# Two heads' scores in turn, masks over 64 rows, and one scaling of all heads of a block

## The chip, the cores and the metric

The kernel runs on one core of one Trainium2 chip. The metric is device time in microseconds (us) of the whole program, the median of several runs. The core's engines are PE (TensorE: matmuls, with its weight loads shown as PEld), DVE (VectorE), ACT (ScalarE), POOL (GpSimd) and SP (SyncE, which issues the DMAs). They run side by side and wait for each other through semaphores; each takes its own instructions in a fixed order.

## The reference

```python
# attention with a memory: q, k, v are (8, 8, 576, 64)
scores = scale * np.matmul(q, k.transpose(0, 1, 3, 2))     # masked: keys after the query are left out
a = np.exp(scores - scores.max(-1, keepdims=True)); a /= a.sum(-1, keepdims=True) + 1e-09
local = np.matmul(a, v)
q_p = phi(q)                                               # x + 1 for x > 0, else exp(x)
mem_out = (q_p @ M_prev) / (q_p . z_prev + 1e-6)           # per head
attn = g * mem_out + (1 - g) * local                       # g = sigmoid(beta), per head
# FFN over all 4608 tokens, 512 -> 2048 -> 512
h = x @ w_in
out = (h * np.clip(h + 3.0, 0.0, 6.0) / 6.0) @ w_out
```

There are 8 sequences of 576 tokens and 8 heads of 64 columns; the FFN's weights come as float64.

## The kernel before

Attention is cut into units. A unit is one head and some 128-query blocks of one sequence: blocks 0 and 1 together, then 2, 3, and 4 (64 queries). A sequence has 32 units, in the order query blocks, pair of heads, head; there are 256. Keys lie on partitions, so a unit's scores fill one PSUM bank `sT`, of which three exist. A unit runs through these steps:

- `scores` (PE): L343 for sequence 0, whose q and k stay float32 with head 0 on partitions 0 to 63 and head 1 on 64 to 127, so that a product uses 64 rows of the array; L347 and L348 for the other sequences, in float16 parts over 128 rows. L350 adds the causal mask to the diagonal block, by a product of an identity with `negm` over 128 rows.
- `reduce`: the largest score per query, on DVE (L360; L358 on ACT for block 0) into `rm`, of which one exists, and then over the partitions on POOL (L362) into `mb`.
- `sub` (DVE, L368) into the tile `a`, of which two exist; `exp` (ACT, L377). From sequence 1 on, POOL makes the float16 upper part `ah` (L381) and DVE the lower `al` (L389, method `lo`).
- `pv` (PE): L407 and L408 for sequence 0, L413 to L417 otherwise. A group `o` in PSUM holds, for a block and both heads of a pair, the product with v, the one with the memory, and the two sums to divide by; two such banks exist.
- `combine`, after the second head of a pair: three small DVE operations make the factors `cf` (L430 to L432), four ACT operations scale the parts out of PSUM (L436, L437), a DVE addition (L438) puts 128 columns of `x` in place, and after the last pair `abs_sum` (L152) adds up magnitudes for the scaling of x.

The FFN works on 18 blocks of 256 tokens, each in 16 pieces: eight of the first product (L523 to L525, or L518 in float32 for block 0), followed by ACT and DVE operations (L531 to L534), and eight of the second (L546 to L548, or L544). Block 0's x is transposed on PE (L505), x of the others by DMA (L496). The weights are decoded from float64 on ACT and DVE (L622 to L626) during sequence 0 and split in float16 parts (L156, L157).

The pairs of the next sequence are prepared in ten steps each (load, magnitudes, scales, parts of k, q, phi(q) and v), whose temporaries come from the pools `hl` (three tiles) and `stg` (three).

The order in which each engine takes its instructions comes from a planner that lays out all instructions in a timeline of its own. An instruction's priority is the piece of the FFN at which it is wanted: `due(t)` for attention, 40 pieces ahead of the FFN (10 in the first 16 units), the piece's own number for the FFN, and fixed ones for the decoding of the weights. Loops only emit instructions; they don't set the order on an engine.

Of the kernel before, what the change touches and what calls it, by code (L numbers as in the profile page):

```python
# [67 lines left out]
def kernel(ctx, tc, qT, kT, v, mz, beta, w_in, w_out, out):  # L68
    nc = tc.nc
    PE, DVE, ACT, POOL, SP = nc.tensor, nc.vector, nc.scalar, nc.gpsimd, nc.sync  # L70
    B, NP, _, S = qT.shape          # 8, 4, 128, 576
    H = 2 * NP
    D = 64
    NT, DM = out.shape              # 4608, 512
    DFF = w_in.shape[1]             # 2048
    NB = 5                          # 128-token tiles per sequence (the last one has 64)
    TB = 256                        # tokens of an FFN block
# [13 lines left out]
    xpool = pool("xpool", XPB)  # L91
    ps_f = pool("ps_f", 2, space=PSUM)
# [11 lines left out]
    nat_eps = const.tile([P, 2], F32, name="nat_eps")  # L104
# [12 lines left out]
    for i in range(NSLOT):  # L117
# [9 lines left out]
        if i < NP:  # L127
            w32 = whole.bitcast(F32)
            nat.append(dict(q=w32[:, 0:S], k=w32[:, S:S + NB * P], qp=w32[:, S + NB * P:2 * S + NB * P],
                            v=w32[:, 2 * S + NB * P:2 * S + NB * P + NB * 130]  # L130
                            .rearrange("p (t h e) -> p t h e", t=NB, h=2)))
        else:
            raw.append(whole[:, 0:4096])

    def at(step):
# [18 lines left out]
    def split(hi, lo, src, s):  # L154
        """hi + lo = src * s, both float16."""
# [4 lines left out]
    slots = {}  # L160

    def prep_steps(b, p):
# [25 lines left out]
        def scale():  # L188
# [7 lines left out]
            DVE.memset(scal[:, 2:3], SA * 1e-9)  # L196
            DVE.tensor_scalar(scal[:, 3:4], s[:, 3:4], 1e-6, mem[b]["s"][:, 1:2], op0=ALU.mult, op1=ALU.mult)
            coef = mem[b]["coef"][:, 2 * p:2 * p + 2]
            DVE.tensor_scalar_mul(coef[:, :, 0], omg[:, 2 * p:2 * p + 2], i[:, 2:3])
            eps = scal[:, 2:4].unsqueeze(1).broadcast_to([P, 2, 2])  # L200
            esc, shift = scal[:, 0:1], scal[:, 1:2]
            slots[b, p] = dict(sl=sl, esc=esc, shift=shift, coef=coef, eps=eps)
# [23 lines left out]
        def do_phi():  # L226
            e = hl.tile([P, S], F32, name=f"e_{b}_{p}", tag="hl")
            q = st["q"][:, :S]
# [17 lines left out]
    def nat_load(p, part):  # L246
        """a pair of heads of sequence 0, for float32 products"""
# [12 lines left out]
    def nat_phi(p, part):  # L260
# [5 lines left out]
        coef = mem[0]["coef"][:, 2 * p:2 * p + 2]  # L266
        slots[0, p] = dict(esc=0.125, shift=8.0 * LN_SA, coef=coef,
                           eps=nat_eps.unsqueeze(1).broadcast_to([P, 2, 2]))

    def nat_mem():  # L270
# [8 lines left out]
        mem[0] = dict(t=m, coef=coef)  # L279
# [3 lines left out]
    def mem_steps(b):  # L283
# [16 lines left out]
        def conv():  # L300
# [7 lines left out]
            mem[b] = dict(t=t, s=s, coef=coef)  # L308
# [4 lines left out]
    # a unit: some 128-query blocks of one head, their scores in one PSUM bank, keys on partitions  # L313
    UNITS = [(0, 1), (2,), (3,), (4,)]
    xtiles = {}
    groups = {}

    class Unit:
# [10 lines left out]

        def scores(self):  # L330
            h = self.h
            if self.b == 0:
                t = nat[self.p]
            else:
                sl = slots[self.b, self.p]["sl"]
            sT = self.sT = ps_s.tile([P, 512], F32, name=f"sT_{self.id}", tag="sT")
            for i, nq, c0, _ in self.blocks:
                q0 = i * P
                for j in range(i + 1):
                    o = sT[:, c0 + j * nq:c0 + (j + 1) * nq]  # L340
                    if self.b == 0:
                        r = slice(D * h, D * h + D)
                        PE.matmul(o, t["k"][r, j * P:(j + 1) * P], t["q"][r, q0:q0 + nq],  # L343
                                  start=True, stop=j < i)
                    else:
# [463 lines left out]
```

## Time and profile before

| | |
|---|---|
| median of 3 runs | 1121.5 us (1119.45, 1121.5, 1121.78) |
| the profiled execution, first to last instruction | 1120.2 us |
| PE busy | 1083.2 us (97%) |
| DVE busy | 930.7 us (83%) |
| ACT busy | 791.1 us (71%) |
| POOL busy | 412.2 us (37%) |
| DMA | 101.39 MB, mean 91 GB/s |

The profiled execution's time is its span, 1120.2 us, which lies 1.3 us under the median and within the runs. Busy shares are unions of an engine's instructions. A matmul's record is longer than the time until the next one may start, so a busy PE says that it never stood idle for long, not that it works at its peak; the chain of waits, which gives to each instruction only the time until the next link, is the better measure of what one costs.

### The profile page before, as it was taken

Reading aid. Unit: us, or ns where it says so; the run is one execution under the profiler, and the core shown is the slowest. Engines: PE = TensorE matmul, PEld = TensorE weight load, DVE = VectorE, ACT = ScalarE, POOL = GpSimd, SP = SyncE. Lnnn points to the kernel's source line nnn. Section 1 sums busy time; section 2 is a strip of 40 time slices with the busy share of each in tenths; the row PEclk is TensorE's granted clock in tenths of the full one; section 3 lists DMA queues with packets and bytes.
Section 4 is the critical chain, followed back from the end, with each engine's and each line's share of the span. In section 5 each row is a group of like instructions: output and inputs, shape, how many; then the busy total and the mean of one; then the engine's idle time right before and its main releaser. Section 6 shows DMA issues by size and latency. Waiting matters only on the chain.

```text
span 1120.2 us, 28768 instructions
## 1 busy us (share of the span) xinstructions
PE 1083.2 (97%) x10736; PEld 797.4 (71%) x10736; DVE 930.7 (83%) x2436; ACT 791.1 (71%) x1880; POOL 412.2 (37%) x544
## 2 busy tenths in 40 slices
PE   8999999999999899999999999999999999999998
PEld 6888767586767667676768576867685868685664
DVE  5999889899899969998999988888799968893321
ACT  5787879677877778787877787668686857563321
POOL 3322223444444433554244533354344433341000
PEclk9999999999999999999999999999999999999999
DMA  8734452333424343315332434233404230101100
GB/s 263 291 100 160 119 135 70 94 91 87 116 84 106 70 118 89 97 45 138 97 76 71 101 96 102 76 92 97 116 22 107 77 69 14 36 5 36 27 13 19
DMA packets 101468, 101.39 MB, mean 91 GB/s; under 512 B 50256, under 2 KB 80976, under 8 KB 101328
## 3 DMA queue, kind: packets, MB, share of 16 engines
q1 hardware_dynamic: 101328, 99.56, 33.1%
q8 instruction: 84, 1.38, 0.5%
q14 instruction: 56, 0.46, 0.1%
HBM read 48.14 MB, written 9.44 MB: 51 GB/s over the span
## 4 chain that ended last, share of the span: by engine, by line
PE 42%; DVE 32%; ACT 8%; issue 8%; DMA 6%; POOL 2%; SPq 1%; DVEq 0%; ACTq 0%; POOLq 0%
DVE a L368 6%; PE po L546 5%; PE po L548 5%; PE po L547 5%; PE ph L523 5%; DVE rm L360 5%; PE ph L524 4%; PE ph L525 4%; DVE al L389 4%; DVE r L532 3%; PE ph L518 3%; DVE g L534 2%; PE sT L343 2%; DVE W L157 2%; POOL mb L362 2%
## 5 line engine op out<-in xcount | busy, mean ns | idle before, releaser
L362 POOL PARTITION_ALL_REDUCE mb<-rm x256 | 251.7, 983 | 336.7 <-DVE rm L360 237.4
L523 PE MATMUL ph<-x,W 128*128 128x256 f16 x1088 | 297.6, 274 | 12.7 <-DVE r L532 7.3
L525 PE MATMUL ph<-x,W 128*128 128x256 f16 x1088 | 297.5, 273 | 0.0
L524 PE MATMUL ph<-x,W 128*128 128x256 f16 x1088 | 297.4, 273 | 0.0
L381 POOL TENSOR_SCALAR_AFFINE_SELECT ah<-a 128x384 f16<-128x384 f32 (+2 forms) x224 | 145.4, 650 | 214.4 <-ACT a L377 105.4
L546 PE MATMUL po<-W,g 128*128 128x512 f16 x544 | 206.6, 380 | 1.9 <-ACT ot L554 1.6
L548 PE MATMUL po<-W,g 128*128 128x512 f16 x544 | 206.5, 380 | 0.8 <-DVE g L534 0.8
L547 PE MATMUL po<-W,g 128*128 128x512 f16 x544 | 206.7, 380 | 0.0
L377 ACT ACTIVATE a<-a,scal 128x384 f32<-128x384 f32 (+2 forms) x224 | 141.6, 633 | 57.0 <-DVE a L368 48.8
L368 DVE SCALAR_TENSOR_TENSOR a<-sT,scal,mb 128x128 f32<-128x128 f32 (+4 forms) x280 | 147.2, 541 | 13.3 <-POOL mb L362 12.4
L360 DVE TENSOR_REDUCE rm<-sT 128x128 f32<-128x256 f32 (+3 forms) x256 | 135.6, 530 | 11.5 <-PE sT L350 4.6
L389 DVE TENSOR_TENSOR al<-a,ah 128x384 f16<-128x384 f32 (+2 forms) x224 | 134.0, 598 | 9.2 <-POOL ah L381 8.0
L532 DVE SCALAR_TENSOR_TENSOR r<-r,ph 128x512 f32<-128x512 f32 x136 | 92.1, 677 | 53.2 <-ACT r L531 52.6
L436 ACT ACTIVATE x<-o,cf 128x64 f32<-128x64 f32 (+1 forms) x320 | 100.6, 314 | 44.2 <-DVE cf L432 39.5
L531 ACT ACTIVATE r<-ph,bias_g,gsc 128x512 f32<-128x512 f32 x136 | 106.5, 783 | 34.2 <-PE ph L525 29.1
L347 PE MATMUL sT<-slot 128*128 128x128 f16 (+1 forms) x840 | 123.7, 210 | 3.9 <-DVE a L368 2.1
L348 PE MATMUL sT<-slot 128*128 128x128 f16 (+1 forms) x840 | 124.3, 210 | 0.0
L523 PEld LDWEIGHTS <-W 128*128 128x128 f16 x1088 | 106.8, 98 | 23.1 <-issue 6.6
L413 PE MATMUL o<-slot,ah 128*128 128x65 f16 (+1 forms) x840 | 116.3, 195 | 6.9 <-ACT y L437 3.6
L533 ACT ACTIVATE g<-r 128x512 f16<-128x512 f32 x136 | 86.4, 636 | 51.2 <-DVE r L532 51.1
L524 PEld LDWEIGHTS <-W 128*128 128x128 f16 x1088 | 106.7, 98 | 19.5 <-issue 5.0
L414 PE MATMUL o<-slot,ah 128*128 128x64 f16 (+1 forms) x840 | 115.4, 195 | 0.0
(149 smaller groups left out, 2387.4 us busy)
## 6 DMA issues: line engine op xcount, KB each, us to landing
slot<-q SPq DMA_DIRECT2D x112, 144.0 KB, 2.5
out<-ot SPq DMA_DIRECT2D x36, 256.0 KB, 2.0
stv<-vn SPq DMA_DIRECT2D x28, 320.0 KB, 3.3
W<-w_in SPq DMA_DIRECT2D x8, 1024.0 KB, 9.5
slot<-w_out SPq DMA_DIRECT2D x8, 1024.0 KB, 4.9
stq<-qT SPq DMA_DIRECT2D x28, 288.0 KB, 3.1
stk<-kT SPq DMA_DIRECT2D x28, 288.0 KB, 3.3
slot<-k SPq DMA_DIRECT2D x112, 72.0 KB, 2.0
```

The lines of the kernel that those rows point to most:

```text
L360: DVE.tensor_reduce(rm[:, m0:m0 + nq], src.rearrange("p (t q) -> p q t", q=nq), axis=AX.X, op=ALU.max)
L362: POOL.partition_all_reduce(mb[:, 0:self.m], rm[:, 0:self.m], P, RMAX)
L368: DVE.scalar_tensor_tensor(a[:, c0:c0 + w].rearrange("p (t q) -> p t q", q=nq), self.sT[:, c0:c0 + w].rearrange("p (t q) -> p t q", q=nq), ...
L377: ACT.activation(a, a, AF.Exp, scale=slots[self.b, self.p]["esc"])
L381: POOL.affine_select(self.ah[:, 0:self.n], a, pattern=[[0, self.n]], compare_op=ALU.is_ge, fill=0.0, base=1, channel_multiplier=0)
L389: DVE.tensor_tensor(self.al[:, 0:n], self.a[:, 0:n], self.ah[:, 0:n], op=ALU.subtract)
L523: PE.matmul(ph[:, m], wh, f["xh"][:, c], start=c == 0, stop=False)
L524: PE.matmul(ph[:, m], wh, f["xl"][:, c], start=False, stop=False)
L525: PE.matmul(ph[:, m], wl, f["xh"][:, c], start=False, stop=c == 3)
L546: PE.matmul(po, gh[:, m, ts], W2[:, m, 0:512], start=m == 0, stop=False)
L547: PE.matmul(po, gh[:, m, ts], W2[:, m, 512:], start=False, stop=False)
L548: PE.matmul(po, gl[:, m, ts], W2[:, m, 0:512], start=False, stop=m == 15)
```

## The change

It has two parts. In sequence 0, the scores of the two heads of a pair are issued together: for each block and key tile a product of head 0 and one of head 1 in turn, into two `sT` banks. Their mask is added by products over 64 rows, two of 64 columns for a block of 128 queries, from the small tiles `selm` and `neg2`, which are built at the start in the free end of a slot. In the second part, `combine` no longer scales: one ACT copy per block and pair brings the whole group `o` into a tile `y` in SBUF, and after the last pair `normalise` makes the factors of all eight heads with three DVE operations and scales head by head, one ACT and one DVE operation each. The constants `eps` and `coef` stand per sequence for all heads, and two operations of a preparation move from DVE to ACT.

To make room, `rm` now stands in the first 256 columns of `a`, which is therefore taken at `reduce`; `hl` has two tiles and `x` three; phi's temporary is the staging tile of k; `y` has two tiles.

```diff
-HLB = 3
-XPB = 4
+HLB = 2
+XPB = 3
...
+        def scores_nat(self, other):
+            t = nat[self.p]
+            us = (self, other)
+            for u in us:
+                u.sT = ps_s.tile([P, 512], F32, name=f"sT_{u.id}", tag="sT")
+            for i, nq, c0, _ in self.blocks:
+                q0 = i * P
+                for j in range(i + 1):
+                    for u in us:
+                        r = slice(D * u.h, D * u.h + D)
+                        PE.matmul(u.sT[:, c0 + j * nq:c0 + (j + 1) * nq], t["k"][r, j * P:(j + 1) * P],
+                                  t["q"][r, q0:q0 + nq], start=True, stop=j < i)
+                for a in range(nq // D):
+                    for u in us:
+                        r = slice(D * u.h, D * u.h + D)
+                        c = c0 + i * nq + a * D
+                        PE.matmul(u.sT[:, c:c + D], selm[r, a, :], neg2[r, a, :],
+                                  start=False, stop=a == nq // D - 1)
...
         def reduce(self):
-            rm = p1.tile([P, 256], F32, name=f"rm_{self.id}", tag="rm")
+            a = self.a = p2.tile([P, 512], F32, name=f"a_{self.id}", tag="a")
+            rm = a[:, 0:256]
...
         def sub(self):
-            a = self.a = p2.tile([P, 512], F32, name=f"a_{self.id}", tag="a")
+            a = self.a
...
-                cf = small.tile([P, 2, 2], F32, name=f"cf_{self.id}_{i}", tag="cf")
-                DVE.tensor_tensor(cf[0:nq], g[0:nq, :, :, D], sd["eps"][0:nq], op=ALU.add)
-                DVE.reciprocal(cf[0:nq], cf[0:nq])
-                DVE.tensor_tensor(cf[0:nq], cf[0:nq], sd["coef"][0:nq], op=ALU.mult)
...
-                for h in range(2):
-                    ACT.activation(xs[:, h * D:(h + 1) * D], g[0:nq, h, 1, 0:D], AF.Copy, scale=cf[0:nq, h, 1:2])
-                    ACT.activation(y[:, h * D:(h + 1) * D], g[0:nq, h, 0, 0:D], AF.Copy, scale=cf[0:nq, h, 0:1])
-                DVE.tensor_tensor(xs, xs, y, op=ALU.add)
...
+                    ytiles[b, i] = ypool.tile([P, H, 2, D + 1], F32, name=f"y_{b}_{i}", tag="y")
+                y = ytiles[b, i]
+                ACT.activation(y[0:nq, 2 * p:2 * p + 2], groups[i][0:nq], AF.Copy)
+            if p == NP - 1:
+                for i, nq, _, _ in self.blocks:
+                    self.normalise(i, nq)
+
+        def normalise(self, i, nq):
+            b = self.b
+            y = ytiles[b, i][0:nq]
+            x = xtiles[b, i] = xpool.tile([P, DM], F32, name=f"x_{b}_{i}", tag="x")
+            cf = small.tile([P, H, 2], F32, name=f"cf_{b}_{i}", tag="cf")[0:nq]
+            DVE.tensor_tensor(cf, y[:, :, :, D], mem[b]["eps"][0:nq], op=ALU.add)
+            DVE.reciprocal(cf, cf)
+            DVE.tensor_tensor(cf, cf, mem[b]["coef"][0:nq], op=ALU.mult)
+            for h in range(H):
+                ACT.activation(y[:, h, 1, 0:D], y[:, h, 1, 0:D], AF.Copy, scale=cf[:, h, 1:2])
+                DVE.scalar_tensor_tensor(x[0:nq, h * D:(h + 1) * D], y[:, h, 0, 0:D], cf[:, h, 0:1],
+                                         y[:, h, 1, 0:D], op0=ALU.mult, op1=ALU.add)
+            abs_sum(amx[0:nq, b * NB + i:b * NB + i + 1], x[0:nq])
+            done_tiles.append((b, i))
...
+    DVE.memset(selm, 0.0)
+    for r in (slice(0, D), slice(D, P)):
+        DVE.tensor_copy(selm[r, 0, 0:D], ident[r, r])
+        DVE.tensor_copy(selm[r, 1, D:P], ident[r, r])
+        r0 = slice(r.start, r.start + 1)
+        DVE.memset(selm[r0, 0, 0:1], 0.0)
+        DVE.memset(selm[r0, 0, D:P], 1.0)
+        for a in range(2):
+            DVE.tensor_copy(neg2[r, a, :], negf[r, r])
+        DVE.memset(neg2[r0, 0, :], -3e38)
```

More of the change, by code (lines that the diff above doesn't have):

```diff
@@ L91 @@
     xpool = pool("xpool", XPB)
+    ypool = pool("ypool", 2)
     ps_f = pool("ps_f", 2, space=PSUM)
@@ L103 @@
     half = const.tile([P, 1], F32, name="half")
-    nat_eps = const.tile([P, 2], F32, name="nat_eps")
+    nat_eps = const.tile([P, H, 2], F32, name="nat_eps")
     W1 = const.tile([P, 17, 1024], F16, name="W1")
@@ L133 @@
             raw.append(whole[:, 0:4096])
+        if i == NP - 1:
+            free = whole.bitcast(BF16)[:, 2 * (2 * S + NB * P + NB * 130):]
+            selm = free[:, 0:2 * P].rearrange("p (a k) -> p a k", a=2)
+            neg2 = free[:, 2 * P:3 * P].rearrange("p (a q) -> p a q", a=2)
     def at(step):
@@ L195, in scale @@
             DVE.tensor_scalar(scal[:, 1:2], s[:, 0:1], s[:, 1:2], 8.0 * LN_SA, op0=ALU.mult, op1=ALU.mult)
-            DVE.memset(scal[:, 2:3], SA * 1e-9)
-            DVE.tensor_scalar(scal[:, 3:4], s[:, 3:4], 1e-6, mem[b]["s"][:, 1:2], op0=ALU.mult, op1=ALU.mult)
+            ACT.activation(mem[b]["eps"][:, 2 * p:2 * p + 2, 1], mem[b]["eps1"], AF.Copy, scale=s[:, 3:4])
             coef = mem[b]["coef"][:, 2 * p:2 * p + 2]
-            DVE.tensor_scalar_mul(coef[:, :, 0], omg[:, 2 * p:2 * p + 2], i[:, 2:3])
-            eps = scal[:, 2:4].unsqueeze(1).broadcast_to([P, 2, 2])
+            ACT.activation(coef[:, :, 0], omg[:, 2 * p:2 * p + 2], AF.Copy, scale=i[:, 2:3])
             esc, shift = scal[:, 0:1], scal[:, 1:2]
-            slots[b, p] = dict(sl=sl, esc=esc, shift=shift, coef=coef, eps=eps)
+            slots[b, p] = dict(sl=sl, esc=esc, shift=shift)
         def pair_tiles(nm):
@@ L226, in do_phi @@
         def do_phi():
-            e = hl.tile([P, S], F32, name=f"e_{b}_{p}", tag="hl")
-            q = st["q"][:, :S]
+            q, e = st["q"][:, :S], st["k"][:, :S]
             ACT.activation(e, q, AF.Relu, scale=-1.0)
@@ L265, in nat_phi @@
         DVE.scalar_tensor_tensor(e, q, 0.0, e, op0=ALU.max, op1=ALU.add)
-        coef = mem[0]["coef"][:, 2 * p:2 * p + 2]
-        slots[0, p] = dict(esc=0.125, shift=8.0 * LN_SA, coef=coef,
-                           eps=nat_eps.unsqueeze(1).broadcast_to([P, 2, 2]))
+        slots[0, p] = dict(esc=0.125, shift=8.0 * LN_SA)
     def nat_mem():
@@ L278, in nat_mem @@
         DVE.tensor_copy(coef[:, :, 1], gate)
-        mem[0] = dict(t=m, coef=coef)
+        mem[0] = dict(t=m, coef=coef, eps=nat_eps)
     mem = {}
@@ L307, in conv @@
             DVE.tensor_scalar(coef[:, :, 1], gate, s[:, 1:2], i[:, 0:1], op0=ALU.mult, op1=ALU.mult)
-            mem[b] = dict(t=t, s=s, coef=coef)
+            eps = small.tile([P, H, 2], F32, name=f"eps_{b}", tag="eps", bufs=2)
+            DVE.memset(eps[:, :, 0], SA * 1e-9)
+            eps1 = small.tile([P, 2], F32, name=f"eps1_{b}", tag="eps1", bufs=2)
+            DVE.tensor_scalar_mul(eps1, s[:, 1:2].broadcast_to([P, 2]), 1e-6)
+            mem[b] = dict(t=t, s=s, coef=coef, eps=eps, eps1=eps1)
         return [load, lambda: None, absmax, conv]
     UNITS = [(0, 1), (2,), (3,), (4,)]
-    xtiles = {}
+    xtiles, ytiles = {}, {}
     groups = {}
@@ L332, in scores @@
             if self.b == 0:
-                t = nat[self.p]
-            else:
-                sl = slots[self.b, self.p]["sl"]
+                if h == 0:
+                    self.scores_nat(self.pair)
+                return
+            sl = slots[self.b, self.p]["sl"]
             sT = self.sT = ps_s.tile([P, 512], F32, name=f"sT_{self.id}", tag="sT")
@@ L340, in scores @@
                     o = sT[:, c0 + j * nq:c0 + (j + 1) * nq]
[L341 to L345, printed above, removed]
-                        kk = kst[sl][:, h, j * P:(j + 1) * P]
-                        PE.matmul(o, kk, qhl[sl][:, 0, h, q0:q0 + nq], start=True, stop=False)
-                        PE.matmul(o, kk, qhl[sl][:, 1, h, q0:q0 + nq], start=False, stop=j < i)
+                    kk = kst[sl][:, h, j * P:(j + 1) * P]
+                    PE.matmul(o, kk, qhl[sl][:, 0, h, q0:q0 + nq], start=True, stop=False)
+                    PE.matmul(o, kk, qhl[sl][:, 1, h, q0:q0 + nq], start=False, stop=j < i)
                     if j == i:
@@ L666 @@
         nat_pads(p)
-    DVE.memset(nat_eps[:, 0:1], SA * 1e-9)
-    DVE.memset(nat_eps[:, 1:2], 1e-6)
+    DVE.memset(nat_eps[:, :, 0], SA * 1e-9)
+    DVE.memset(nat_eps[:, :, 1], 1e-6)
     ACT.activation(gate, beta_sb, AF.Exp, scale=-1.0)
@@ L699 @@
     NU = len(units)
+    for t in range(0, NU, 2):
+        units[t].pair = units[t + 1]
     upb = NU // B
```

9 lines of the change are left out of this document (removed).

## The prediction

> **What bounds the kernel now.** I read the page's busy shares first, then the windows by stage, then the chain of waits in the stage that the change touches most, then groups by form.
>
> ```profile
> span 1120.2 us, 28768 instructions
> PE 1083.2 (97%) x10736; PEld 797.4 (71%) x10736; DVE 930.7 (83%) x2436; ACT 791.1 (71%) x1880; POOL 412.2 (37%) x544
> 0.00:64.00 64.00, 58.34 (x237) 49.34 (x237) 49.82 (x132) 43.47 (x106) 21.57 (x25) 1.00 0.74 243
> 64.00:151.00 87.00, 86.87 (x500) 68.15 (x499) 78.77 (x192) 70.41 (x153) 22.81 (x24) 1.00 0.48 138
> 151.00:280.00 129.00, 120.34 (x1268) 86.54 (x1266) 119.09 (x311) 100.31 (x243) 54.28 (x70) 1.00 0.35 92
> 420.00:560.00 140.00, 136.73 (x1535) 102.54 (x1534) 132.16 (x365) 112.44 (x274) 60.09 (x80) 1.00 0.35 93
> 1000.00:1121.00 121.00, 114.44 (x865) 74.14 (x862) 37.97 (x83) 39.86 (x76) 6.07 (x11) 0.99 0.10 23
> ```
>
> The windows give length, then busy PE, PEld, DVE, ACT, POOL. From 64 us on PE is never idle for long: 86.87 of 87 us, later 93 to 98%. DVE is close behind (92% in 151 to 280, 94% in 420 to 560) until attention ends near 1000 us, and after that PE alone works. So PE work that disappears shortens the run, if DVE and the attention's buffers keep up; DVE work that disappears helps only through PE's waits.
>
> The chain from 64 to 151 us, sequence 0 beside FFN block 0, says the same:
>
> ```profile
> by line: PE ph L518 33.9%; PE sT L343 24.5%; PE o L407 16.4%; PE po L544 16.1%; PE o L408 3.6%; PE sT L350 2.8%; DVE a L368 1.1%; SPq L211 0.6%; SPq L210 0.6%; issue 0.3%; SPq L496 0.2%; DVE cf L432 0.1%; DVEq L368 0.0%
> 64.50 1.65 PE sT L343 x6
> 75.79 0.86 PE sT L343 x6
> 94.41 1.08 PE sT L343 x8
> 138.10 1.25 PE sT L343 x10
> 147.56 0.81 PE sT L343 x6
> 64.00:151.00 87.00, 23.64 (x150) 19.20 (x150) 1.00 0.48 138
> ```
>
> PE carries nearly all of it. L343, the scores of sequence 0, holds 24.5% of 87 us = 21.3 us, its mask (L350) 2.4 us. Columns are start, time on the chain, what; the last row is the window again, for L343 alone (its 150 matmuls and weight loads). Six instructions took 1.65 us at 64.5 but 0.86 at 75.8: in the first 70 us TensorE ran at half the speed, whatever the page's clock column (which says 1.00) shows.
>
> **Scores of sequence 0.** Read the cost of one from the chain: (1.08 - 0.86)/2 = 0.11 us per instruction, and 0.86 - 6 x 0.11 = 0.20 us to begin a piece. In the 64-column form of the last block (1.25 - 0.81)/4 is again 0.11, though the operand that streams is half as long. So what sets 0.11 there is not the streaming but, as far as the trace shows, the weight load that each instruction brings; and the 0.20 comes each time the array goes from 128-row work to these 64-row instructions.
>
> The change issues the two heads alternately, on partitions 0 to 63 and 64 to 127, into two PSUM banks, and keeps the mask at 64 rows too. Two terms:
> - 25 L343 pieces on the chain between 64 and 151 us (first 64.50, last 147.56, both above) become eight or nine pairs, some split. About 12 beginnings at 0.18 go: -2 us.
> - 150 instructions (the count in that window) at 0.11 = 16.5 us. If the two halves of the array work side by side this is 8.3 us less; if not, nothing. No row shows two halves at once. I take three quarters, -6, because of the 64-column form: an instruction whose streaming fills half its slot leaves the array waiting on its own half's weights.
>
> The Trainium skill, "TensorEngine Tiling (Array Packing)", Key Properties, says that tiles run weight loads and matmuls in parallel and that a change of tiling mode drains the engine; by it the second term is the full -8.3. The 0.20 us agrees with the drain; the parallel part no trace here shows. "TensorE: Matmul & The Clock Gate", Part 3, says that a weight load overlaps a running matmul only when the row group differs; 0.11 us for the 128-column form with one row group, loading and streaming in turn with no more than that between two starts, speaks against the word "only".
>
> The mask goes from one 128-column instruction per block and head to two of 64 columns. Before 17 of them took the 2.4 us, 0.14 each; after, an estimate of 0.1 per block in the same mode: -1 us; bounds -2 and +1. Scores together: -9 us, between -1 and -12. The scores before 64 us get cheaper too, but what PE waits for there is the x of FFN block 0 (last part); they count in the bounds of that step alone.
>
> The 15 small DVE instructions that build the masks come at the very start, where DVE is least busy (49.82 of 64 us in that window, most of it later). Nothing, or 1 us if the first mask waits.
>
> **Copies and scaling.**
>
> ```profile
> L437 ACT ACTIVATE y<-o,cf 128x64 f32<-128x64 f32 x256 | 82.6, 323 | 0.0
> L436 ACT ACTIVATE x<-o,cf 128x64 f32<-128x64 f32 x256 | 81.3, 317 | 35.6 <-DVE cf L432 30.8 <-DVE cf L431 2.0 <-PE sT L350 1.8
> L438 DVE TENSOR_TENSOR x<-x,y 128x128 f32<-128x128 f32 x128 | 39.6, 313 | 7.3 <-ACT y L437 7.0
> L432 DVE TENSOR_TENSOR cf<-cf,coef 128x4 f32<-128x4 f32 x128 | 27.4, 222 | 0.5
> L431 DVE RECIPROCAL cf<-cf 128x4 f32<-128x4 f32 x128 | 20.3, 167 | 0.4
> L430 DVE TENSOR_TENSOR cf<-o,scal 128x4 f32<-128x4 f32 x112 | 16.1, 151 | 6.6 <-PE o L417 6.4
> L199 DVE TENSOR_SCALAR coef<-omg,i 128x2 f32<-128x2 f32 x28 | 7.5, 268 | 0.0
> L197 DVE TENSOR_SCALAR scal<-s,s_m 128x1 f32<-128x1 f32 x28 | 5.6, 200 | 0.0
> L358 ACT ACTIVATE rm<-sT 128x128 f32<-128x128 f32 x64 | 17.8, 278 | 6.1 <-POOL mb L362 3.7 <-PE sT L350 2.2
> L377 ACT ACTIVATE a<-a,scal 128x320 f32<-128x320 f32 x56 | 31.3, 560 | 18.6 <-DVE a L368 14.5 <-POOL ah L381 2.5 <-DVE cf L432 1.1
> L377 ACT ACTIVATE a<-a,scal 128x512 f32<-128x512 f32 x56 | 40.5, 724 | 15.3 <-DVE a L368 12.4 <-DVE cf L432 1.9 <-DVE cf L431 0.7
> 41.94 0.20 ACT x L436
> PE o L413 <- ACT y L437: 3.6, 6, 1.3
> PE sT L347 <- DVE cf L430: 1.5, 1, 1.5
> PE ph L523 <- DVE r L532: 7.3, 7, 2.5
> ```
>
> DVE before: 151 + 167 + 222 + 313 = 853 ns for each of 160 pair-blocks, 136 us. After, for 40 blocks: three operations on 16 columns (0.55 us) and eight 64-column ones, for which there is no row; between 222 (L432) and 313 (L438, twice as long), nearer L438 as these have a pointer too: 290. 0.55 + 2.32 = 2.87 us, 115 us in all (93 to 122). With 28 x (200 + 268) = 13 us moved from the preparation to ACT, DVE loses about 34 us of 930.
>
> ACT before: four scalings, of which each holds the chain for 0.20 us (row at 41.94; they overlap), 0.8 x 160 = 128 us. After: one copy of 260 columns, 278 + 132 x (724 - 560)/192 = 391 ns, 63 us; eight scalings from SBUF per block, between 0.20 (that spacing) and 560 - 256 x 0.854 = 341 ns, say 0.25, 80 us; 56 small ones in the preparation, at that same 0.20, 11 us. ACT gains about 26 us and stays below 80%, so no cost by itself.
>
> What reaches PE: the waits for the output banks (3.6 us, L413 behind L437) and for cf (1.5) go, since a bank is free after one copy; what is late next is the 7.3 us in which PE waits for r, which DVE's relief trims a little and the new bursts (a block's eight pairs of operations in a row, two blocks at once for the first unit) lengthen. Net -5 + 3 = -2 us, between -8 and +8.
>
> **The shared tile a.** The maxima now stand in a, so a is taken at the reduction, not at the subtraction, and two exist.
>
> ```profile
> 91.16 1.11 PE L407 MATMUL o<-slot,a 128*128 128x65 f32 x8
> 86.69 0.67 DVE L360 TENSOR_REDUCE rm<-sT 128x128 f32<-128x512 f32 x1
> 93.36 0.67 DVE L368 SCALAR_TENSOR_TENSOR a<-sT,mb 128x512 f32<-128x512 f32 x1
> 100.59 1.11 PE L407 MATMUL o<-slot,a 128*128 128x65 f32 x8
> 447.44 0.55 DVE L360 TENSOR_REDUCE rm<-sT 128x128 f32<-128x384 f32 x1
> 447.91 0.55 DVE L389 TENSOR_TENSOR al<-a,ah 128x384 f16<-128x384 f32 x1
> 453.18 0.55 DVE L389 TENSOR_TENSOR al<-a,ah 128x384 f16<-128x384 f32 x1
> L362 POOL PARTITION_ALL_REDUCE mb<-rm x256 | 251.7, 983 | 336.7 <-DVE rm L360 237.4
> ```
>
> In sequence 0 the reduction at 86.69 ran 5.6 us before the product at 91.16 that frees its tile had ended (92.27); now it must follow, and with 0.67 + 0.98 + gaps its subtraction moves from 93.36 to about 94.3 to 94.9. The product it feeds started only at 100.59, PE having been given other work, so about 6 us cover this. Later the reduction at 447.44 starts 1.0 us before L389 two units earlier ends (448.46). It and its own L389 (end 453.73) lie 6.3 us apart: 3.15 us per unit with two tiles, against an average pace of about 1000/256 = 3.9 (attention fills the windows up to 1000 us, and L362 runs once per unit). That fits; behind a waiting reduction stand DVE's FFN operations, though. I take 0 as the cover exists; without it +1.5 us for each of ten rounds of sequence 0.
>
> **First x.** FFN block 0 waits for its x:
>
> ```profile
> 57.68 0.28 DVE L438 TENSOR_TENSOR x<-x,y 128x128 f32<-128x128 f32 x1
> 63.74 0.63 PE L505 MATMUL xp<-ident,x 128*128 128x128 f32 x2
> 66.16 2.45 PE L518 MATMUL ph<-x,W 128*128 128x256 f32 x5
> ```
>
> Of eight transposes only the last two (the row at 63.74) had to wait for the last pair; now all do (six more at about 0.2 us, 1.3 us), and for its scaling, whose 5.7 us replace 6.8 us spread earlier. +2 us (-3 to +5).
>
> The other edits: two hl tiles are enough since e moved to the staging tile, which is then kept two steps longer; one x tile less, but x is now taken only when finished. Cover: the steps of a preparation lie a unit, some 3.9 us, apart. SP's DMAs are the same in number; I count 0.
>
> **Sum.** 1120.2 - 9 - 2 + 0 + 2 = 1111.2 us of span; the median of the runs is 1.3 us above this span: 1112.5.
>
> **Rivals.**
> - Halves do not overlap: the second term is 0 and scores give -3; with -2 and +2 the run ends at 1118.5 or, with the bounds of the first x, 1116 to 1123. For it: 0.11 us looks set by weight loads, which have one queue. The same would be seen if the alternation only saved beginnings.
> - The tile a decides (slower). If the product is not 6 us but under 1.5 us behind the subtraction, each of ten rounds of sequence 0 costs 1.5 to 2 us, FFN block 0 runs out before x of block 1 is there, and in the sequences after it reductions stand 1 us late with DVE's queue behind them. 20 us of late attention less the 9 saved: 1121.5 + 11 = 1132. It decides once a unit's hold on a exceeds 2 x 3.9 us; 6.3 speaks against it, DVE at 94% for it.
> - DVE's relief counts fully: the 7.3 us of waits for r shrink too (-5 instead of -2), scores give -12, x is 3 us early: 1120.2 - 12 - 5 - 3 + 1.3 = 1101.5.
>
> **Chances.** Forecast 0.43 (own range 1106 to 1119), halves do not overlap 0.24, a decides 0.24, full relief 0.09. Repeats lie within 0.2% (1119.45 to 1121.78), which is what a measurement can tell from no change. Faster: 0.42 + 0.09 + a quarter of the second case = 0.56; same: half of the second and a little, 0.15; slower 0.29. Eight in ten: 1101 to 1132.
>
> **What would show it.** L343 pairs on the chain near 0.06 us per instruction: the overlap; 0.11: rival one. Subtractions of sequence 0 more than 1.5 us later after the product two units before, and a gap on PE between the last L544 and the first L523: rival two. ACT copies near 0.39 and 64-column DVE operations near 0.29 us check the copies. L518 starting in earnest after 70 us would break the first-x step; PE idle over 50 us between 151 and 840 would break the steady one.

## The result, and the profile after

The changed kernel takes 1131.24 us (median of 4 runs, 1129.75 to 1132.64), the kernel before 1120.47 us in the same comparison: ratio 1.0102, 95% interval 1.0082 to 1.0122. It is 1% slower; faster was forecast, 1112.5 us. The profiled execution has a span of 1128.0 us against 1120.2.

The page of the changed kernel (span, busy time by engine, the chain's shares by engine):

```profile
span 1128.0 us, 28530 instructions
PE 1078.5 (96%) x10768; PEld 795.4 (71%) x10768; DVE 925.4 (82%) x2181; ACT 797.4 (71%) x1776; POOL 400.1 (35%) x544
PE 44%; DVE 27%; ACT 10%; issue 8%; DMA 6%; POOL 3%; SPq 2%; DVEq 0%; ACTq 0%; POOLq 0%
PE po L575 5%; PE po L574 5%; PE po L573 5%; PE ph L550 5%; PE ph L551 5%; PE ph L552 5%; DVE a L382 4%; DVE a L390 4%; DVE al L411 4%; PE ph L545 3%; DVE r L559 2%; DVE x L465 2%; DVE g L561 2%; ACT y L464 2%; ACT a L399 2%
```

Busy totals hardly moved. The place of the loss is seen by stage. Windows of the kernel before and then of the changed one, cut at 228 and 242 us, where FFN block 2 begins (length, then busy PE, PEld, DVE, ACT, POOL, granted clock, DMA share, GB/s):

```profile
0.00:64.00 64.00, 58.34 (x237) 49.34 (x237) 49.82 (x132) 43.47 (x106) 21.57 (x25) 1.00 0.74 243
64.00:151.00 87.00, 86.87 (x500) 68.15 (x499) 78.77 (x192) 70.41 (x153) 22.81 (x24) 1.00 0.48 138
228.00:242.00 14.00, 14.00 (x184) 12.35 (x183) 14.00 (x29) 10.41 (x23) 6.59 (x8) 1.00 0.62 168
242.00:1000.00 758.00, 739.04 (x8327) 545.58 (x8325) 682.59 (x1817) 565.40 (x1378) 326.53 (x442) 1.00 0.32 81
```

```profile
0.00:64.00 64.00, 47.93 (x234) 44.14 (x234) 46.14 (x125) 40.64 (x92) 18.35 (x23) 1.00 0.73 243
64.00:151.00 87.00, 83.80 (x464) 65.96 (x465) 77.42 (x165) 70.10 (x145) 21.61 (x23) 1.00 0.44 133
228.00:242.00 14.00, 9.87 (x114) 7.83 (x113) 13.40 (x29) 9.52 (x19) 6.48 (x9) 0.76 0.54 139
242.00:1000.00 758.00, 739.64 (x8293) 544.58 (x8291) 674.56 (x1602) 569.42 (x1297) 316.99 (x438) 1.00 0.31 83
```

PE is busy 10.4 us less before 64 us, 3.1 less from there to 151, and another 4.1 less around 235 us, where the mean granted clock is 0.76. From 242 to 1000 us the two do alike. The start of FFN block 2 says it in one figure: its first product starts at 236.1 us against 227.8, 8.3 us later, and from there to the end both need 892 us (1128.0 - 236.1, 1120.2 - 227.8). Between these two executions the whole loss arises before block 2. PE's timeline of the kernel before and then of the changed one (in brackets the wait and what ended it):

```profile
227.81 0.27 PE L523 MATMUL ph<-x,W 128*128 128x256 f16 x1 [1.43 <-DMA x<-W]
```

```profile
236.05 0.37 PE L550 MATMUL ph<-x,W 128*128 128x256 f16 x1 [0.36 <-DMA x<-W]
```

Block 1's last product ends at 226.3 us before and at 228.3 now, so block 2 follows it after 1.5 us before and after 7.8 us now. In these 7.8 us PE does bits of attention until x of block 2 has come.

Two things are late there. First, attention of sequence 0. Windows again, for the products of its probabilities with v alone (PE, PEld; the trace has two instructions for each float32 product, 240 in all, and I count instructions here and below), of the kernel before (L407) and of the changed one (L429):

```profile
64.00:125.00 61.00, 12.08 (x88) 10.83 (x88) 1.00 0.43 138
```

```profile
64.00:125.00 61.00, 9.49 (x65) 8.76 (x65) 1.00 0.43 138
```

With those of the first 64 us (72 and 66), 160 have begun by 125 us before and 131 after. Unit 31 of sequence 0 ends at 178.2 us instead of 164.7. Second, x of FFN block 0. The waits of the changed kernel from 36 to 85 us (engine, line, releaser; us in total, times, longest) and PE's timeline there:

```profile
PE xp L532 <- DVE x L465: 3.7, 1, 3.7
DVE a L382 <- PE o L429: 2.4, 1, 2.4
```

```profile
62.17 0.63 PE L532 MATMUL xp<-ident,x 128*128 128x128 f32 x2
66.52 0.90 PE L532 MATMUL xp<-ident,x 128*128 128x128 f32 x3 [3.71 <-DVE x L465]
75.21 3.34 PE L545 MATMUL ph<-x,W 128*128 128x256 f32 x8
```

The transposes stand still for the scaling of all heads. Four instructions of block 0's products need only half of them; from the fifth on, all are needed. The fifth is my mark for the start of block 0: 75.2 us, against 66.2 before.

The parts of the change by themselves: the groups of the changed kernel (count, busy us, mean ns, idle before), and the chain of waits from 64 to 151 us.

```profile
L465 DVE SCALAR_TENSOR_TENSOR x<-y,cf 128x64 f32<-128x64 f32 (+1 forms) x320 | 75.8, 293 | 1.3 <-ACT y L464 1.2
L449 ACT ACTIVATE y<-o 128x260 f32<-128x260 f32 (+1 forms) x160 | 57.6, 376 | 37.4 <-PE o L439 32.2 <-PE o L430 3.8 <-DVE x L465 1.2
L346 PE MATMUL sT<-slot 64*128 64x128 f32 (+1 forms) x240 | 45.4, 352 | 14.9 <-DMA slot<-qT 4.4 <-issue 4.4 <-DVE a L390 3.4
```

```profile
82.69 0.03 PE sT L352
83.76 0.13 PE sT L352
84.84 0.06 PE sT L352 x2
93.32 1.09 PE sT L346 x8
97.53 0.86 PE sT L346 x6
105.50 0.64 PE sT L346 x4
```

Copy (376 ns) and scaling (293 ns) cost what was estimated. An instruction of the scores still takes (1.09 - 0.64)/4 = 0.11 us on the chain, as before: mostly, the two heads' products do not overlap. In the order that the planner gave to PE, one head's products mostly stand in a row and the other's follow later. A mask (L352) takes 0.03 us behind scores and 0.13 where it begins a piece.

### The profile page after: what moved, and what is told of

It reads as the page before. It is cut to its first block, busy times and chain, and to the rows that moved or that the text cites. A ratio compares the mean times of both kernels' runs of the same rounds, so it can differ in the third digit from the quotient of the medians.

```text
span 1128.0 us, 28530 instructions
## 1 busy us (share of the span) xinstructions
PE 1078.5 (96%) x10768; PEld 795.4 (71%) x10768; DVE 925.4 (82%) x2181; ACT 797.4 (71%) x1776; POOL 400.1 (35%) x544
## 4 chain that ended last, share of the span: by engine, by line
PE 44%; DVE 27%; ACT 10%; issue 8%; DMA 6%; POOL 3%; SPq 2%; DVEq 0%; ACTq 0%; POOLq 0%
PE po L575 5%; PE po L574 5%; PE po L573 5%; PE ph L550 5%; PE ph L551 5%; PE ph L552 5%; DVE a L382 4%; DVE a L390 4%; DVE al L411 4%; PE ph L545 3%; DVE r L559 2%; DVE x L465 2%; DVE g L561 2%; ACT y L464 2%; ACT a L399 2%
## 5 line engine op out<-in xcount | busy, mean ns | idle before, releaser
L384 POOL PARTITION_ALL_REDUCE mb<-a x256 | 239.2, 938 | 312.1 <-DVE a L382 247.6
L403 POOL TENSOR_SCALAR_AFFINE_SELECT ah<-a 128x384 f16<-128x384 f32 (+2 forms) x224 | 138.1, 617 | 247.6 <-ACT a L399 221.5
L399 ACT ACTIVATE a<-a,scal 128x384 f32<-128x384 f32 (+2 forms) x224 | 138.7, 622 | 61.5 <-DVE a L390 49.5
L411 DVE TENSOR_TENSOR al<-a,ah 128x384 f16<-128x384 f32 (+2 forms) x224 | 131.7, 589 | 27.8 <-POOL ah L403 26.8
L382 DVE TENSOR_REDUCE a<-sT 128x128 f32<-128x256 f32 (+3 forms) x256 | 135.9, 533 | 15.2 <-ACT a L380 6.6
L368 PE MATMUL sT<-slot 128*128 128x128 f16 (+1 forms) x840 | 120.4, 211 | 6.0 <-DVE a L390 5.1
L550 PEld LDWEIGHTS <-W 128*128 128x128 f16 x1088 | 106.6, 98 | 22.6 <-issue 4.4
L369 PE MATMUL sT<-slot 128*128 128x128 f16 (+1 forms) x840 | 121.6, 211 | 0.0
L551 PEld LDWEIGHTS <-W 128*128 128x128 f16 x1088 | 106.5, 98 | 16.0 <-issue 1.3
L552 PEld LDWEIGHTS <-W 128*128 128x128 f16 x1088 | 106.6, 98 | 11.8
```

Source lines behind the costliest of these rows:

```text
L382: DVE.tensor_reduce(rm[:, m0:m0 + nq], src.rearrange("p (t q) -> p q t", q=nq), axis=AX.X, op=ALU.max)
L384: POOL.partition_all_reduce(mb[:, 0:self.m], rm[:, 0:self.m], P, RMAX)
L399: ACT.activation(a, a, AF.Exp, scale=slots[self.b, self.p]["esc"])
L403: POOL.affine_select(self.ah[:, 0:self.n], a, pattern=[[0, self.n]], compare_op=ALU.is_ge, fill=0.0, base=1, channel_multiplier=0)
L411: DVE.tensor_tensor(self.al[:, 0:n], self.a[:, 0:n], self.ah[:, 0:n], op=ALU.subtract)
L550: PE.matmul(ph[:, m], wh, f["xh"][:, c], start=c == 0, stop=False)
```

## The experiments

Theory A: the scaling of all heads at once makes the first x of a sequence late (A2: of every sequence, not only the first). Theory B: tile `a`, taken at the reduction, slows attention. Rivals: the scores issued in pairs cost by themselves (C); the smaller pools cost (D); the order of issue costs, whatever the work (O). Each kernel's ratio is to the kernel before, with its 95% interval, from runs on the same chip.

**The parts alone.** e1_scores is the kernel before with the scores and masks of the change only.

> The first part of the change alone (scores of sequence 0 issued per pair of heads, masks over 64 rows), put into the kernel before; scaling, tiles and pools as before. Theory A (the loss is the late first x: scaling all heads at once holds up FFN block 0 by 9 us): nothing of that is in here, so 1118 to 1121 us, with the first long row of L518 at 64 to 67 us. Theory B (the tile a, taken at the reduction, slows the attention of sequence 0): the same, 1118 to 1121. Theory C (issuing the pair's scores together costs by itself, the second head waiting for a bank): 1125 or more, first FFN products later than 70 us.

1123.84 us, ratio 1.0029 (1.0013 to 1.0045), a time that none of the three had given. The part that was to bring 9 us costs 3. By 125 us 160 products have begun, like in the kernel before, so up to there attention runs neither slower nor faster. Block 2 starts at 226.8 us, 1.0 earlier than before: what this part costs lies after it.

e2_scaling is the rest of the change, with the scores of before.

> The second part alone: unscaled copies, scaling of all heads at once, with all that makes room for it (maxima in a, two hl tiles, three x tiles); scores and masks as in the kernel before. Theory A: all of the loss, 1129 to 1133 us, first dense FFN products at 73 to 77 us. Theory B: the same time. Theory C: 1119 to 1123 us.

1128.97 us, 1.0074 (1.0059 to 1.0089): most of the loss. e3_room takes only what made room: the maxima in `a`, two `hl` tiles, phi's temporary in the staging tile of k.

```diff
-            rm = p1.tile([P, 256], F32, ...)
+            a = self.a = p2.tile([P, 512], F32, ...)
+            rm = a[:, 0:256]
...
-HLB = 3
+HLB = 2
-            e = hl.tile([P, S], F32, ...)
+            q, e = st["q"][:, :S], st["k"][:, :S]
```

> Only what makes room: maxima in the first columns of a, hl with two tiles, phi's temporary in k's staging tile (x keeps four tiles, since it is taken at the first pair here); scaling per pair and scores as before. Theory A: no loss, 1119 to 1122 us, first FFN products at 64 to 68 us, though subtractions of sequence 0 come later. Theory B: 1127 to 1131 us, with the attention of sequence 0 some 10 us late at its end. Theory C: 1119 to 1122.

1129.66 us, 1.0081 (1.0066 to 1.0096). The room alone, without any of the new arithmetic, costs as much as e2.

e5_early is the changed kernel with blocks 0 and 1 of sequence 0 scaled pair by pair again.

```diff
+            if b == 0 and self.u == 0:      # four ACT scalings and a DVE addition per pair, from PSUM
+                ...
+                return
```

> The changed kernel with one exception: blocks 0 and 1 of sequence 0 are scaled pair by pair out of PSUM as in the kernel before, all other blocks at once. Theory A: FFN block 0 gets its x early again, dense products from 65 to 68 us, and the time falls by 7 to 10 us to 1120 to 1124. Theory B: the attention stays late, 1128 to 1132. Theory C: 1128 to 1132.

1134.10 us, 1.012 (1.0105 to 1.0135), and block 0's products still start at 74.0 us. Late scaling of the first x is not what holds the changed kernel, as long as everything else stays; theory A by itself falls. The time is 2 us above what theory B gave.

**Tile a.** e7_max_in_a has only the first part of e3's edit, e8_hl only the others.

> One edit to the kernel before: the maxima stand in the first columns of a, which is thereby taken at the reduction. Theory B (tile a): nearly all that the room cost, 1126 to 1131 us, block 0 of the FFN ending at 150 to 155 us while the product of unit 23 ends at 140 us or later (125.0 before), and PE without FFN work in between. Theory D (the loss of the room came from the two hl tiles or from phi's temporary): 1119 to 1122 us.

> The rest of the room alone: two hl tiles and phi's temporary in k's staging tile; the maxima in their own tile as before. Theory B: 1119 to 1122 us. Theory D: 1126 to 1131 us.

e7: 1135.94 us, 1.0136 (1.0104 to 1.0168). e8: 1121.43 us, 1.0000 (0.9985 to 1.0015). So the pools by themselves are free, and what the room costs comes with tile `a`. The parts don't add up, though: e7 is one of e3's edits and costs more than e3 (1.0081), and more than the whole change. Then e14_a3 gives e7 a third tile `a`.

```diff
-            a = self.a = p2.tile([P, 512], F32, name=f"a_{self.id}", tag="a")
+            a = self.a = p2.tile([P, 512], F32, name=f"a_{self.id}", tag="a", bufs=3)
```

> Kernel before with the maxima reduced into tile a (as in e7_max_in_a, which was 1.36% slower) but with three tiles a instead of two. Theory B (the ring of two tiles a is what the early taking costs): the third buffer gives the two rounds of cover back, so within 0.3% of before (1117 to 1124 us), and attention of sequence 0 as before (unit 23 ended near 121 to 129 us against 142.8 in e7). Rival (e7 was slow for the order of issue that the planner made of it, not for the ring): still 1130 to 1138 us.

1121.91 us, 0.9995 (0.9977 to 1.0013): the cost is gone. The windows of the products with v, as above, of e7 and then of e14:

```profile
0.00:64.00 64.00, 17.85 (x66) 16.28 (x66) 1.00 0.74 243
64.00:125.00 61.00, 7.47 (x54) 6.80 (x54) 1.00 0.43 138
```

```profile
0.00:64.00 64.00, 18.02 (x72) 16.52 (x72) 1.00 0.74 243
64.00:125.00 61.00, 11.22 (x80) 10.33 (x80) 0.92 0.37 124
```

120 products by 125 us against 152. The ring of two tiles, held from the reduction on, is a cause, and it is shown on the unchanged arithmetic. The start of block 2 does not show it: 237.0 us in e7, 237.2 in e14. But in e7 it is 9.5 us after block 1's end, in e14 0.8 us, and in e14 attention is further on by then (48 instructions of line L416, the lower parts' products with v, against 36), so that less is left to do: 882.4 us from there to the end against 897.3. The start of block 2 is a good mark of lateness only beside these two.

**Does the array overlap two heads?** e6_forced_scores is e1 with the alternation fixed on PE.

```diff
+            def mm(*args, **kw):            # each product of the two heads is issued after the one before
+                with tc.issue_after(last[0].ins):
+                    last[0] = PE.matmul(*args, **kw)
```

> The kernel with the scores' part alone, with each score product of a pair and each mask product bound to follow the one before it in the order of issue, head 1 first, so that the two halves of the array really alternate on PE (in the changed kernel's own order the heads mostly come one after the other). If the halves work side by side: near 0.06 us per L343-type instruction (0.55 us for a pair's first 8), and 1112 to 1119 us. If weight loads keep them in turn: 0.11 us each as before, and 1119 to 1126 us, PE waiting where a second bank comes late.

1131.27 us, 1.0093 (1.0059 to 1.0127). PE's timeline of the changed kernel (one head) and then of e6 (two heads in turn), eight instructions of 128 columns each:

```profile
81.54 1.16 PE L346 MATMUL sT<-slot 64*128 64x128 f32 x8
```

```profile
100.25 0.72 PE L348 MATMUL sT<-slot 64*128 64x128 f32 x8
```

Eight take 0.72 us instead of 1.16. In e6's trace they start two by two, 7 ns apart, one for each half of the array, and 0.11 us lie between two such pairs. So the halves work side by side, PE does the scores nearly twice as fast, and the kernel is still 0.9% slower, slower than either expectation: unit 23 ends at 149.5 us, against 125.0 before. A likely reason, which I did not test, is that a pair now starts only when two `sT` banks are free at once. PE's time was not what attention lacked.

**The cure of B in the changed kernel.** e9_after_mb reduces the maxima in place in `mb` and takes `a` at the subtraction again.

```diff
-            a = self.a = p2.tile([P, 512], F32, ...)
-            rm = a[:, 0:256]
             mb = self.mb = p2.tile([P, 256], F32, ...)
+            rm = mb
```

> The changed kernel with the maxima written into mb and reduced there in place, so that a is taken at the subtraction again; all else as changed. Theory B: most of the loss goes, 1119 to 1125 us, unit 23's product ends before 132 us (141.1 in the changed kernel). If the scaling at once or the pair of scores were the cost instead: 1128 to 1133 us.

1134.63 us, 1.0137 (1.009 to 1.0183). Attention of sequence 0 is fast again (180 products by 125 us, the fifth instruction of block 0 at 61.3 us), and nothing is gained: the waits have moved. Here theory B alone falls too. e13_mb does this edit on the kernel before, e10_scaling_mb on e2.

> Kernel before with the maxima reduced into tile mb and the all-reduce done in place, so that the single tile rm no longer makes a reduction wait for the all-reduce before it; tile a as before. If e9_after_mb was slow for this way of holding the maxima: 1126 to 1136 us here too. If it was slow for the scaling of all heads at once: here 1115 to 1122 us, same as before or up to 0.4% faster, with unit 31 of sequence 0 ended near 155 us as in e9 (154.1; before 164.7).

> Copies and scaling of all heads at once alone (e2_scaling) with the maxima in mb instead of a; scores as before. Theory B alone (tile a was all that e2 lost): 1117 to 1123 us. Theory A2 (scaling all heads at once makes the x of the first tiles of every sequence late, so that FFN block 2 starts near 237 us instead of 228, and similar gaps follow at later sequences): 1127 to 1134 us, as e9.

e13: 1129.21 us, 1.0061 (1.0038 to 1.0083), so holding the maxima in `mb` costs the kernel before 0.6%, which I had not expected. e10: 1134.70 us, 1.0135 (1.0096 to 1.0175), 0.7% beyond e13. Scaling at once costs something where `a` does not hold attention back. e12_pairs_mb tests that: e9, but blocks 0 and 1 of every sequence scaled pair by pair out of PSUM (four tiles `x`, one `y`).

```diff
+            if self.u == 0:
+                ...
+                    ACT.activation(xs_h, g[0:nq, h, 1, 0:D], AF.Copy, scale=cf[0:nq, h, 1:2])
+                    DVE.scalar_tensor_tensor(xs_h, g[0:nq, h, 0, 0:D], cf[0:nq, h, 0:1], xs_h, ...)
+                return
```

> e9_after_mb with blocks 0 and 1 of every sequence scaled pair by pair straight from PSUM, as the kernel before does, and the other blocks all heads at once (four tiles x, one tile y). Theory A2: the first x of a sequence comes early again, FFN block 2 starts before 230 us, and the time is 1118 to 1126 us. Rival (many small waits of another order of issue, none of them the first x): 1130 to 1136 us as e9, whatever block 2 does.

1115.96 us, 0.9943 (0.9921 to 0.9965): 18.7 us less than e9, faster than the kernel before, and 2 us below what theory A2 gave. The window at block 2 of e9 and then of e12:

```profile
228.00:242.00 14.00, 9.97 (x82) 6.83 (x81) 13.12 (x26) 7.93 (x19) 7.59 (x7) 0.76 0.67 160
```

```profile
228.00:242.00 14.00, 12.67 (x164) 10.46 (x162) 13.54 (x23) 9.94 (x17) 8.40 (x9) 1.00 0.59 148
```

Block 2 holds the last 64 tokens of sequence 0 and the first 192 of sequence 1, so it needs x of that sequence's first two query blocks. It starts at 236.8 us in e9 and 231.8 in e12, 6.3 and 1.1 us after the end of block 1. In the 16 us up to block 4 and up to block 13, in each of which the first query block of another sequence is wanted, PE waits for 3.5 and 3.6 us in e9, for 0.4 and 0.2 in e12. So scaling at once does delay blocks, where attention isn't late already. That is theory A2, with two reserves: the tiles `x` and `y` changed in number along with it, and these delays are the smaller part of the gain. The expected mark, block 2 before 230 us, was missed, and from block 2 to the end e12 needs 879.8 us against 897.6 in e9 and 892.4 in the kernel before. Why the rest is so much shorter is open; 11 us of it are less idle time of PE (11.8 us after the start of block 2 against 22.8).

**Both undone, and each put back.** e16_pairs_rm is e12 with `rm` as a tile of its own again; e18_pairs_a has the maxima in `a`; e19_pairs_noscores is e16 with the scores of before.

> e12_pairs_mb with the maxima in a tile rm of their own again, as in the kernel before; so the changed kernel with both suspected costs undone: tile a is taken at the subtraction, and blocks 0 and 1 of every sequence are scaled pair by pair from PSUM (one tile y, four tiles x). Theory (A2 and B are what the change lost, and mb in place cost 0.6% in e13): 1105 to 1114 us, 0.6 to 1.4% faster than before. Rival (e12 gained by a lucky order of issue): 1116 to 1125 us.

> e16 with the maxima in tile a (two of them) as in the changed kernel. Theory B: some 1.0 to 1.4% slower than e16, 1118 to 1130 us, attention of sequence 0 late (unit 23 ended after 138 us). Rival (with the rest cured, PE has cover enough): within 0.4% of e16.

> e16 with the scores and masks of sequence 0 as in the kernel before. If the scores part gains nothing or loses its 0.3% (e1_scores): 0 to 0.4% faster than e16. If the cheaper masks gain here what they could not in e1: 0.2 to 0.5% slower than e16.

e16: 1124.69 us, 1.0028 (1.0012 to 1.0044). e18: 1131.01 us, 1.0083 (1.0063 to 1.0103). e19: 1141.13 us, 1.0171 (1.0136 to 1.0207). B holds again: 6.3 us between e16 and e18, 160 products by 125 us against 121. e18 is no faster than the changed kernel (1131.24), so with `a` as it is the early scaling is worth nothing, as in e5. (Of e19's runs, 1134 to 1147 us, the profiled one is the shortest.) All three expectations failed in part. e16 does not beat the kernel before, and e12's way of holding the maxima, which cost e13 0.6%, is worth 8.7 us here. The difference of e18 to e16 is 0.6%, where 1.0 to 1.4 was expected. And the scores part, which costs 0.3% alone, gains 1.4% in e16 over e19. In e19 block 2 starts at 241.3 us (231.0 in e16), with PE and its clock down:

```profile
228.00:242.00 14.00, 6.68 (x82) 4.96 (x82) 13.69 (x31) 10.21 (x22) 7.97 (x9) 0.71 0.40 92
```

```profile
228.00:242.00 14.00, 12.70 (x153) 10.69 (x151) 14.00 (x26) 10.14 (x17) 8.76 (x11) 0.80 0.57 140
```

**Is it the order of issue?** Three kernels with the same work and another order: the kernel before with 41 pieces of lead (e21_order_lead) or the preparation two pieces later (e22_order_po), and the changed one with 41 (e23_after_order).

```diff
-LEAD = 40
+LEAD = 41
```

> Kernel before with one figure of the order of emission altered: attention runs 41 pieces of the FFN ahead instead of 40. The same instructions and tiles; about half of the streams of all engines stand in another order. If the planner's order alone scatters the time of this kernel by some 0.5% (theory O): anywhere from 1115 to 1132 us, more than 0.2% from before. If order alone is worth little: 1118 to 1123 us.

> Kernel before with the preparation of the next pairs two pieces later (10 instead of 8), everything else equal. Theory O: 1115 to 1132 us, more than 0.2% from before, in either direction. If order alone is worth little: 1118 to 1124 us.

> The changed kernel with 41 pieces of lead instead of 40. If its loss is a matter of the order that the planner came to: between 1118 and 1138 us, off from 1131.2 by more than 3 us. If the loss is in the tiles (theory B and the late x): 1129 to 1133 us, whatever the order, and unit 23 of sequence 0 still ends after 138 us, block 2 of the FFN after 234 us.

Ratios 0.9988 (0.9968 to 1.0008), 1.0002 (0.9985 to 1.0019) and 1.0115 (1.0082 to 1.0149). Although about half of PE's instructions stand elsewhere in the first two, neither differs from the kernel before, and e23 keeps the loss with its marks: 132 products by 125 us, block 2 at 237.3 us. (Its time, 1134.25 us, is 1 us above the range given for a loss in the tiles, but the ratio agrees with the changed kernel's 1.0102.) These small shifts of order are worth 0.2% at most on the kernel before. The loss goes with the tiles.

| kernel | ratio | products with v by 125 us | block 1 ends, us | block 2 starts, us | from there to the end, us |
|---|---|---|---|---|---|
| before | 1 | 160 | 226.3 | 227.8 | 892.4 |
| changed | 1.0102 | 131 | 228.3 | 236.1 | 891.9 |
| e1, scores alone | 1.0029 | 160 | 225.1 | 226.8 | 896.3 |
| e7, maxima in a | 1.0136 | 120 | 227.5 | 237.0 | 897.3 |
| e14, three tiles a | 0.9995 | 152 | 236.4 | 237.2 | 882.4 |
| e9, cure of B | 1.0137 | 180 | 230.5 | 236.8 | 897.6 |
| e12, e9 scaled early | 0.9943 | 170 | 230.7 | 231.8 | 879.8 |
| e16, both cures | 1.0028 | 160 | 219.9 | 231.0 | 889.2 |
| e18, a put back | 1.0083 | 121 | 226.7 | 236.0 | 893.4 |

## Why the prediction was wrong, step by step

- **What bounds the kernel.** "PE work that disappears shortens the run, if DVE and the attention's buffers keep up" failed before 228 us, by its condition. PE is nearly always busy there, but FFN block 0 and attention share it, and block 2 cannot start before x of sequence 1, whose way leads through DVE, ACT, POOL and DMAs. In e16 block 0's last second product ends at 158.7 us, 11 us earlier than the 169.7 of before, yet block 1 starts only at 165.4 and block 2 at 231.0: what PE gained it waited out.
- **Scores, -9 us.** The step that failed is "the change issues the two heads alternately". The loops emit them so; the planner mostly did not keep it. So 0.11 us stayed, the sign of the first rival, though not for its reason: the disputed overlap itself is real (0.72 us for eight in e6). Instead of -9 us the part alone measured +3 (e1), and where the overlap was forced, +11 (e6). The Trainium skill, "TensorEngine Tiling (Array Packing)", Key Properties, lets tiles load and multiply in parallel: e6 agrees, at (0.72 - 0.27)/7 = 0.064 us between starts, where 0.27 us is one record of the kind in e6; two of them, on different halves, start 7 ns apart. The Trainium skill, "TensorE: Matmul & The Clock Gate", Part 3, lets a weight load overlap a running matmul only in another row group, and e6 beside the 0.11 us of one row group fits that too. No row shows how long a load or a stream takes by itself, so the 0.11 us, which the prediction held against the word "only", is no evidence against it. The mask term was right: 0.03 us in most places and 0.13 at the start of a piece, against 0.14 before.
- **Copies and scaling, -2 us.** The prices held: 376 ns for the copy (391 forecast), 293 for DVE's 64 columns (290), some 0.25 us between ACT's scalings. DVE's relief did not: 34 us forecast, 930.7 - 925.4 = 5.3 us measured. I had added mean durations, but short records overlap their neighbours, as DVE's timeline of the kernel before shows (start, length, count):

```profile
301.58 0.22 DVE L430 TENSOR_TENSOR cf<-o,scal 128x4 f32<-128x4 f32 x2
301.77 0.25 DVE L431 RECIPROCAL cf<-cf 128x4 f32<-128x4 f32 x2
301.98 0.24 DVE L432 TENSOR_TENSOR cf<-cf,coef 128x4 f32<-128x4 f32 x2
302.14 0.35 DVE L368 SCALAR_TENSOR_TENSOR a<-sT,scal,mb 128x128 f32<-128x128 f32 x1
```

  Six operations fill 302.14 - 301.58 = 0.56 us, 0.09 each, where the groups' means (151, 167 and 222 ns) gave 1.08. ACT rose by 6.3 us (26 forecast), in the main for the same reason: of the 57.6 us of the new copies, other records of ACT cover 18.
- **Tile a, 0 us.** This is the step that turned the sign. Alone it measured +15.5 us (e7), and 6.3 us between e16 and e18. Rival two had the mechanism. That its 1132 us is the time measured is luck: it is a sum of 20 us of late attention, where 13.5 were measured at unit 31, less 9 us saved by the scores, which never came. "About 6 us cover this" took one wait for slack. In sequence 0 the rows that I quoted give a hold from the subtraction at 93.36 to the end of the product at 100.59 + 1.11 = 101.70, 8.3 us, already beyond the 2 x 3.9 us at which I had said that it decides; the 6.3 us that "speaks against it" came from the float16 units at 447 us. (By the pace of sequence 0 itself, 5.0 us per unit over its last eight, two tiles allow 10.0 us; with reduction and all-reduce the hold is 8.3 + 0.67 + 0.98 = 9.95 us, at the limit without any gap.) With reduction and all-reduce in the hold the ring sets the pace. The traces show it unit by unit: from the third unit of sequence 0 on, the kernel before starts 23 of 30 reductions before the product two units earlier has ended; the changed kernel, e7 and e18 start none of the 30 before it, and e14, with three tiles, 22. For unit 15 of the changed kernel:

```profile
82.65 0.88 PE L429 MATMUL o<-slot,a 128*128 128x65 f32 x6
85.87 0.55 DVE L382 TENSOR_REDUCE a<-sT 128x128 f32<-128x384 f32 x1
```

  Unit 13's product ends at 82.65 + 0.88 = 83.53 us, and the reduction that takes its tile follows. 32 units add the delays up: 13.5 us at unit 31. A late product is then late for the next unit too, so PE being elsewhere covers nothing. What is not shown is how much of the changed kernel's own loss this is: curing it there by `mb` (e9) gained nothing, and the cure that e16 uses was not run without the early scaling.
- **First x, +2 us (-3 to +5).** Measured +9.0 us in the changed kernel, out of the range, by the fifth instruction of block 0. In e2, without the scores part, it is 67.9 - 66.2 = +1.7 as forecast. The difference comes from parts together, not from the scaling burst: e5 takes the burst away and starts at 74.0 us, e9 frees `a` and starts at 61.3. What the sum left out is what else DVE has to do: on the changed kernel's chain from 57.5 to 66.5 us, when the last transposes become free, the decoding of weights (L650 to L652) stands between the scalings and takes 6.3 us, the scalings 2.1.
- **Rest of the run, 0.** Right, 891.9 us from block 2 on against 892.4, but with some luck: in the kernels of the table, which have nearly the same work there, this stretch takes from 879.8 to 897.6 us.
- **Chances.** Those for faster add up to 0.42 + 0.09 + 0.06 = 0.57, not 0.56.

Not settled: why holding the maxima in `mb` costs 0.6% in e13 and gains 0.8% between e16 and e12, and why the scores part gains 1.4% in e16 and loses 0.3% in e1. In all of them PE's work is nearly the same and what differs is how long it stands before blocks 1 and 2 and later; which resource is last there I did not isolate. The granted clock may have a part in it: in the profiled executions it is 0.996 in the kernel before and 0.994 in e1, 0.991 in e13, 0.995 in e12, 0.992 in e16 and 0.988 in e19, lower for the slower one each time. Nor was the changed kernel run with three tiles `a`.

## What to carry to other kernels

Count how long a tile of a ring is held, in the stage where it is held longest, against the number of tiles times the pace of that stage; moving its allocation one step earlier is a change of pace, even when no engine gets more work. A gain for the engine that looks busiest counts only up to the next thing that waits for another path: check the first consumer after it (here block 2's x) before adding it to the sum. And where a planner orders the instructions, the order in which loops emit them proves nothing about overlap; read the order on the engine.

## What the runs showed of the hardware

Waits of PE can cost more than their length. Windows of the changed kernel around block 2, columns as above:

```profile
228.00:229.00 1.00, 0.68 (x9) 0.39 (x7) 1.00 (x3) 1.00 (x3) 0.57 (x2) 1.00 0.00 0
229.00:230.00 1.00, 0.23 (x2) 0.11 (x2) 1.00 (x4) 0.27 (x1) 0.46 (x1) 1.00 0.28 68
230.00:231.00 1.00, 0.94 (x18) 0.83 (x18) 0.98 (x3) 0.62 (x1) 0.28 (x1) 1.00 0.28 67
231.00:232.00 1.00, 0.24 (x3) 0.11 (x2) 1.00 (x5) 0.97 (x3) 0.92 (x2) 0.82 1.15 259
232.00:235.00 3.00, 1.13 (x14) 0.97 (x15) 3.00 (x6) 3.00 (x7) 1.12 (x1) 0.50 0.46 138
235.00:238.00 3.00, 2.63 (x17) 1.81 (x15) 3.00 (x6) 1.72 (x4) 1.52 (x2) 0.50 0.40 96
238.00:242.00 4.00, 4.00 (x57) 3.61 (x56) 3.43 (x8) 1.95 (x4) 1.60 (x3) 0.94 0.82 214
```

PE was busy for 2.1 of the 4 us from 228 to 232, in pieces, with no wait over 0.84 us in its timeline there, yet the granted clock fell to 0.50 for 6.8 us, from 231.6 on; two score products that start 0.055 us apart at 230 us start 0.105 apart at 235. The kernel before, busy for all of 228 to 242 us, kept 1.00. So a stage that PE merely limps through is paid a second time, a term that the forecast did not have. Here it is small: PE was busy for some 4 of the 6.8 us, so by my estimate half of that, 2 us, went to the clock. The Trainium skill, "TensorE: Matmul & The Clock Gate", Part 1, has the clock fall after an idle window of about 3.4 us, and tells of a kernel that lost it by frequent short idling; here it was many short waits.

The half speed at the start, which the clock column does not show, is no fixed stretch of 70 us. The instructions of block 0's products start 0.43 us apart until 70.9 us in the kernel before, until 77.9 in the changed one, and 0.21 apart after that; in e12 they are at 0.21 by 61.4 us.
